# A gated decode step: gate moved into the attention output, MLP part added in PSUM, result copied by two engines and stored from two tiles

## The chip, the cores and the metric

The kernel runs on one core of a Trainium2 chip. The metric is device time in microseconds (us) of one execution; lower is better. Each quoted time is the median of a kernel's runs. Times inside an execution are counted from the start of its profile's span, which is some 1.8 us shorter than the device time of the same run.

## The reference

One decode step for 8 batch rows. Two branches are mixed by a gate per row:

```python
x = A_x                                               # [8, 1, 448]
g = sigmoid((x * gate_w).sum(-1, keepdims=True))      # one gate per batch row
a = attention(x, last 1024 keys and values) @ wo      # 16 query heads, 8 kv heads, width 256
b = gelu(layernorm(x) @ w1 + b1) @ w2 + b2
return g * a + (1 - g) * b
```

Almost all of the time goes into reading the keys and the values: 8 rows x 8 heads x 1024 x 256 in bf16, 33.6 MB each, and some 10 MB of weights.

## The kernel before

The cache is processed in 16 units `u`, one for each batch row and half of the kv heads. SyncE loads keys and values through a ring of 9 buffers of 2 MB. What the change touches lies at the start (gate), in `finish` (one small copy for each unit) and in the end after the last keys. Some words used below: PSUM is the memory in which TensorE adds up its products, and a bank is one of the pieces that it is divided into. A semaphore is a counter by which an engine or a DMA tells others that it has finished. A transfer is issued by an engine's queue and lands, that is, has finished, some time later.

```python
def norm_and_gate():
    ...                                             # gg[:, 0] = g, gg[:, 1] = 1 - g, on 8 partitions
    gp = ps_misc.tile([P, 2], F32, tag="misc", name="gp")
    nc.tensor.matmul(gp[:], lhsT=spread[:].rearrange("p i b -> p (i b)"), rhs=gg[:], start=True, stop=True)
    nc.vector.tensor_copy(gg_s[:], gp[:])           # both gates at partitions 32*i + b, i = 0..3

def finish(u):                                      # once for each unit
    ...                                             # two float32 matmuls into sm
    nc.scalar.copy(oT[...], sm[:])                  # L534

def mlp_out(hs):
    ...                                             # MLP output in bb, 4 column blocks at partitions 32*i
    nc.scalar.activation(mixb[:], bb[:], ACT.Copy, scale=gg_s[:, 1:2])   # (1 - g) * b, long before the end

# the end, u is the last unit
turn(u)                                             # VectorE transposes the probabilities: E -> ET
total(u)                                            # TensorE: den
invert(u)
nc.vector.memset(A_ps[:], 0.0)
...
spread_rows(0, HALF)                                # TensorE: pp; VectorE: oP
values(u)                                           # TensorE: PO <- ET, last value block
gather(u); finish(u)
project(0)                                          # 32 small matmuls into A_ps, column blocks at partitions 32*i
spread_rows(HALF, NHQ)
for q in range(1, NHQ):
    project(q)                                      # 96 more
nc.vector.scalar_tensor_tensor(                     # res = g * A_ps + mixb, all 128 partitions at once
    res[:], in0=A_ps[:], scalar=gg_s[:, 0:1], in1=mixb[:], op0=ALU.mult, op1=ALU.add)
for i, (src, cols) in enumerate(tiles(res)):        # 4 blocks of 8 rows x 112 columns
    eng = nc.sync if i % 2 == 0 else nc.scalar
    eng.dma_start(out_f[:, cols], src)
```

## Time and profile before

| | |
|---|---|
| Median device time | 190.97 us (190.83 to 191.34, 5 runs) |
| Span of the profile | 189.3 us |
| Loads | 77.7 MB |
| Projection's end to end of last store issue | 1.07 us |

(The ends of matmuls are modelled in a profile. By "projection's end" I mean, here and below, the start of the first instruction that reads the finished sum, 185.93 us in this profile.)

The page of the profile cuts the span into 40 slices; a digit is a busy share in tenths (9 is 90% or more), PEclk is the granted TensorE clock in tenths, and GB/s is what the DMA engines moved.

```profile
PEclk9999999999699966999955897999858999756955
DMA  5999999999999999999999999999999999999980
GB/s 188 422 424 434 428 435 431 422 422 440 429 433 429 426 436 426 429 436 433 429 426 433 428 436 422 433 433 426 436 426 433 436 426 426 436 433 426 410 356 14
```

The DMA row reads 9 from the second slice to the last but two, and still 8 (356 GB/s) in the last but one. This kernel is bound by its loads, so compute can be expected to cost time only at the start and at the end. The chain of waits that ended last says the same (shares of the span):

```profile
DMA 84%; PE 8%; DVE 3%; ACT 1%; SPq 1%; issue 1%; ACTq 0%
```

So the end has to be read instruction by instruction. In the timeline the columns are: start, duration (both us), engine, line, operation, output and inputs, shapes, count; in brackets the idle time before it and what ended it. (An engine's name with q is its sequencer: an issue or a wait, not work.)

```profile
178.50 0.21 ACT L534 CAST oT<-fin 128x16 bf16<-128x16 f32 x1
178.64 0.71 DVE L471 STREAM_TRANSPOSE ET<-E 128x512 int32<-128x512 int32 x1 [1.18 <-ACT E L458]
178.66 0.30 PEld L482 LDWEIGHTS den<-rowsum,rowden 128*128 128x128 f32 x2 [0.53 <-ACT E L458]
...
178.97 0.34 PE L656 MATMUL pp<-oT,ident 128*32 128x32 bf16 x16
...
179.40 1.04 PE L501 MATMUL PO<-slot,ET 128*16 128x512 bf16 x16
179.42 0.15 DVE L648 MEMSET A_ps<- 128x112 f32 x1
...
181.60 1.02 PE L531 MATMUL fin<-rsel,os__1552 128*128 128x8 f32 x4 [1.16 <-DVE os__1552 L516]
...
182.56 0.92 PE L672 MATMUL A_ps<-slot,oP 128*8 128x112 bf16 x32
...
183.41 2.46 PE L672 MATMUL A_ps<-slot,oP 128*8 128x112 bf16 x96
...
185.93 0.33 DVE L690 SCALAR_TENSOR_TENSOR res<-A_ps,gg_s,mixb 128x112 bf16<-128x112 f32 x1 [1.93 <-PE A_ps L672]
186.29 0.71 SPq L700 DMA_DIRECT2D out_dram<-res  x2
186.29 0.65 ACTq L700 DMA_DIRECT2D out_dram<-res  x2
```

The last value product (PO, 179.40) starts 0.05 us after VectorE has turned the probabilities (178.64 + 0.71). The projection (A_ps) runs from 182.56 to 185.9 without a gap. Then come one VectorE instruction of 0.33 us, and two stores on each of two queues, whose issue takes 0.3 to 0.4 us each. After that the stores land, SyncE waits for them and for everything else, and the program ends.

For the cost of the small copies I looked up the groups by line. Columns: minimum, median and maximum ns, first and last start.

```profile
L534 ACT CAST oT<-fin x16: 215/227/230, 51.7 to 182.7; 128x16 bf16<-128x16 f32 x16
```

SyncE's own waits at the end (line 726 is the end of the program; total us, number of waits, longest):

```profile
SPq L726 <- DMA out_dram<-res: 1.1, 2, 0.9
SPq L726 <- PEq L726: 0.7, 2, 0.5
```

### The profile page before, as it was taken

The page shows a single profiled execution, that of the slowest core. Times are in us where ns is not written, and L with a number is a line of the kernel's source. Part 1 is how long each engine was busy: PE and PEld are TensorE (multiplying, and loading weights), DVE is VectorE, ACT ScalarE, POOL GpSimd, SP SyncE. Part 2 cuts the span into 40 slices and gives each one's busy share as a digit, 9 for nine tenths or more (in the row PEclk, how much of TensorE's full clock was granted, in tenths as well). Part 3 has the DMA queues.
Part 4 walks back from the last instruction along what each step waited for, and adds up shares of the span by engine and source line. Part 5 has one row for each costly group of instructions (what it writes and reads, how often), then busy time and mean ns, then how long its engine had stood idle before and what let it go on. Part 6 is the DMA issues. An engine that isn't in the chain of part 4 may idle for free.

```text
span 189.3 us, 2502 instructions
## 1 busy us (share of the span) xinstructions
PE 134.2 (71%) x1013; PEld 69.8 (37%) x1022; DVE 128.1 (68%) x186; ACT 43.1 (23%) x91; POOL 5.0 (3%) x7
## 2 busy tenths in 40 slices
PE   0036899894878588866669985977499839399772
PEld 0021784441434143424225431533153414153461
DVE  7866266995949494949494949494958686772610
ACT  2031220313040404040401340314004404004510
POOL 8100000000000000000000000000000000000000
PEclk9999999999699966999955897999858999756955
DMA  5999999999999999999999999999999999999980
GB/s 188 422 424 434 428 435 431 422 422 440 429 433 429 426 436 426 429 436 433 429 426 433 428 436 422 433 433 426 436 426 433 436 426 426 436 433 426 410 356 14
DMA packets 6733, 77.84 MB, mean 411 GB/s; under 512 B 945, under 2 KB 1346, under 8 KB 1986
## 3 DMA queue, kind: packets, MB, share of 16 engines
q1 hardware_dynamic: 6512, 77.67, 96.5%
q8 instruction: 7, 0.11, 0.2%
q10 hardware_dynamic: 210, 0.02, 0.1%
q14 instruction: 4, 0.03, 0.0%
HBM read 77.68 MB, written 0.01 MB: 410 GB/s over the span
## 4 chain that ended last, share of the span: by engine, by line
DMA 84%; PE 8%; DVE 3%; ACT 1%; SPq 1%; issue 1%; ACTq 0%
DMA slot<-in_A_k_cache_dram 77%; DMA slot<-in_A_wq_dram 7%; PE S L429 3%; PE A_ps L672 2%; PE PO L501 2%; DVE kt L357 1%; PE fin L531 1%; ACT E L458 1%; SPq L118 1%; DVE mx L441 1%; ACT first L510 1%; DVE ET L471 0%; SPq L134 0%; PE mz L449 0%; DVE os__1552 L516 0%
## 5 line engine op out<-in xcount | busy, mean ns | idle before, releaser
L357 DVE STREAM_TRANSPOSE kt<-slot 128x2048 int32<-128x2048 int32 x32 | 73.7, 2306 | 33.7 <-DMA slot<-in_A_k_cache_dram 33.7
L429 PE MATMUL S<-kt,qw 128*128 128x512 bf16 x256 | 72.9, 433 | 30.5 <-DVE kt L357 26.7
L429 PEld LDWEIGHTS <-qw 128*128 128x128 bf16 x256 | 27.0, 106 | 69.4 <-issue 49.4
L458 ACT ACTIVATE E<-S,nmx 128x1024 bf16<-128x1024 f32 x16 | 22.2, 1387 | 2.6 <-DVE nmx L455 2.6
L534 ACT CAST oT<-fin 128x16 bf16<-128x16 f32 x16 | 3.6, 226 | 79.8 <-PE fin L531 79.8
L501 PE MATMUL PO<-slot,ET 128*16 128x512 bf16 x256 | 20.0, 441 | 0.1
L441 DVE TENSOR_REDUCE mx<-S 128x1 f32<-128x1024 f32 x16 | 19.0, 1187 | 0.3 <-PE S L429 0.3
L510 ACT ACTIVATE first<-PO,own 128x256 f32<-128x256 f32 x16 | 7.6, 473 | 29.2 <-PE PO L501 28.2
L471 DVE STREAM_TRANSPOSE ET<-E 128x512 int32<-128x512 int32 x16 | 11.2, 697 | 2.2 <-ACT E L458 2.2
L449 PE MATMUL mz<-m,same 128*128 128x4 f32 x32 | 6.8, 284 | 4.2 <-ACT oT L534 4.1
L423 PE MATMUL S<-place,foreign 128*128 128x512 bf16 x23 | 9.4, 409 | 0.1
L482 PEld LDWEIGHTS den<-rowsum,rowden 128*128 128x128 f32 x32 | 7.3, 234 | 3.9 <-issue 1.7
L449 PEld LDWEIGHTS mz<-m,same 128*128 128x128 f32 x32 | 5.7, 219 | 6.1 <-ACT oT L534 5.3
L501 PEld LDWEIGHTS <-ET 128*16 128x16 bf16 x256 | 5.3, 94 | 5.5 <-issue 2.3
L423 PEld LDWEIGHTS <-foreign 128*128 128x128 bf16 x32 | 3.2, 99 | 9.7 <-issue 7.9
L482 PE MATMUL den<-rowsum,rowden 128*128 128x1 f32 x32 | 5.2, 232 | 0.4 <-ACT E L458 0.4
L414 DVE CAST qw<-qp 32x512 bf16<-32x512 f32 x4 | 2.7, 687 | 3.4 <-ACT qw L412 3.4
L371 PE MATMUL Sq<-slot,xT 128*8 128x512 bf16 x32 | 3.9, 616 | 1.5 <-DMA slot<-in_A_wq_dram 1.5
L493 ACT ACTIVATE rsel<-sel,rb 128x8 f32<-128x8 f32 x16 | 4.7, 295 | 1.1 <-DVE rb L492 1.1
L455 DVE TENSOR_REDUCE nmx<-mz 128x1 f32<-128x4 f32 x16 | 2.3, 146 | 3.5 <-PE mz L449 3.5
L292 POOL MEMSET qw<- 128x5120 bf16 x1 | 4.4, 4364 | 0.0
L443 DVE TENSOR_SCALAR m<-block,mx 128x4 f32<-128x4 f32 x16 | 3.7, 229 | 0.6
(135 smaller groups left out, 84.9 us busy)
## 6 DMA issues: line engine op xcount, KB each, us to landing
slot<-in_A_v_cache_dram SPq DMA_DIRECT2D x16, 2048.0 KB, 36.5
slot<-in_A_k_cache_dram SPq DMA_DIRECT2D x15, 2048.0 KB, 38.8
slot<-in_A_wo_dram SPq DMA_DIRECT2D x3, 896.0 KB, 30.7
slot<-in_A_k_cache_dram SPq DMA_DIRECT2D x2, 1024.0 KB, 7.1
slot<-in_A_wq_dram SPq DMA_DIRECT2D x1, 2048.0 KB, 11.5
slot<-in_B_w_dram SPq DMA_DIRECT2D x1, 1568.0 KB
slot<-in_B_w_dram SPq DMA_DIRECT2D x1, 1344.0 KB
slot<-in_A_wq_dram SPq DMA_DIRECT2D x1, 1024.0 KB, 13.2
```

The costliest lines, as they stand in the source:

```text
L292: nc.gpsimd.memset(qw[:], 0.0)
L357: nc.vector.transpose(kt[:].rearrange("p c k x r -> p (c k x r)").bitcast(WORD), kn[:, hf * CH * Dh : (hf + 1) * CH * Dh].bitcast(WORD),)
L423: nc.tensor.matmul(S[u][:, cols], lhsT=foreign[:], rhs=place[:], start=True, stop=False)
L429: nc.tensor.matmul(S[u][:, cols], lhsT=qw[:, j, u, m * RQ : m * RQ + P], rhs=kt[:, :, k, :, par], start=False, stop=(k == NK - 1 and par = ...
L441: nc.vector.reduce_max(mx[:], S[u][:], axis=AXIS.X)
L449: nc.tensor.matmul(mz[:], lhsT=same[:], rhs=m4[:], start=True, stop=True)
L458: nc.scalar.activation(E[:].rearrange("p c x i -> p c i x"), S.pop(u)[:].rearrange("p (c i x) -> p c i x", i=PAIR, x=BLK), ACT.Exp, bias=n ...
L471: nc.vector.transpose(ET[:].rearrange("p c r i -> p (c r i)").bitcast(WORD), E[:].rearrange("p c x i -> p (c x i)").bitcast(WORD),)
L482: nc.tensor.matmul(den[u][:], lhsT=rowden[:], rhs=rowsum[:], start=True, stop=True)
L493: nc.scalar.activation(rsel[u][:], sel2[:], ACT.Copy, scale=rb[:])
L501: nc.tensor.matmul(PO[32 * t : 32 * t + PAIR * RQ], lhsT=ET[:, c, 0:RQ, :], rhs=vn[:, PAIR * c * Dh : PAIR * (c + 1) * Dh], start=(c < QUA ...
L510: nc.scalar.activation(first[:], PO[:, 0, :], ACT.Copy, scale=own[:, 0:1])
```

## The change

The intent: take the combining instruction out of the end. The gate is multiplied into the attention output while that is copied per unit anyway (a row's gate has to stand on all 128 partitions for this, hence the second small matmul at the start). The MLP's part is added by TensorE, as an identity matmul that opens the sum in `A_ps`. What is left at the end are copies; they are dealt out to two engines, and write two tiles of 8 rows, so that two stores are enough instead of four. Buffers of the MLP are shared to pay for the new constants, and the pad is cut so that the ring stays in its place.

```diff
+    each = consts.tile([NB, NB + P], F32); ident_f = consts.tile([P, P], F32)      # (two lines, shortened)
-    res = consts.tile([P, DO], BF16)
+    res = [consts.tile([NB, D // 2], BF16, name=f"res{i}") for i in range(2)]
 ... norm_and_gate: the gate of every row on all partitions
+        nc.vector.memset(each[:], 1.0)
+        nc.vector.tensor_scalar_mul(each[:, 0:NB], ident[0:NB, 0:NB], gg[:, 0:1])
+        nc.tensor.matmul(
+            gp[:, 1 : 1 + NB], lhsT=each[:, NB : NB + P], rhs=each[:, 0:NB], start=True, stop=True
+        )
 ... finish
-        nc.scalar.copy(oT[...], sm[:])
+        nc.scalar.activation(oT[...], sm[:], ACT.Copy, scale=gg_s[:, 1 + b : 2 + b])
 ... the end
-    nc.vector.memset(A_ps[:], 0.0)
+    nc.tensor.matmul(
+        A_ps[:], lhsT=ident_f[:], rhs=mixb[:], start=True, stop=False, skip_group_check=True
+    )
 ... project
-                    start=(q == 0 and j == 0),
+                    start=False,
 ... result
-    nc.vector.scalar_tensor_tensor(res[:], in0=A_ps[:], scalar=gg_s[:, 0:1], in1=mixb[:], ...)
-    for i, (src, cols) in enumerate(tiles(res)):
-        eng = nc.sync if i % 2 == 0 else nc.scalar
-        eng.dma_start(out_f[:, cols], src)
+    for i, (part, cols) in enumerate(tiles(A_ps)):
+        copy = nc.vector.tensor_copy if i < 2 else nc.scalar.copy
+        copy(res[i // 2][:, (i % 2) * DO : (i % 2 + 1) * DO], part)
+    for i, eng in ((0, nc.sync), (1, nc.scalar)):
+        eng.dma_start(out_f[:, i * D // 2 : (i + 1) * D // 2], res[i][:])
```

More of the change, by code (lines that the diff above doesn't have):

```diff
@@ L179, in slot @@
         return slots[index[key]]
-    consts.tile([P, 448], BF16, name="pad")
+    consts.tile([P, 16], BF16, name="pad")
     x_sb = consts.tile([NB, D], BF16)
@@ L228 @@
     spread = consts.tile([NB, OT, P // OT], F32)
-    gg_s = consts.tile([P, 2], F32)
+    gg_s = consts.tile([P, 1 + NB], F32)
+    ident_f = consts.tile([P, P], F32)
+    each = consts.tile([NB, NB + P], F32)
     ones_r = consts.tile([1, NB], BF16)
     mixb = consts.tile([P, DO], F32)
-    res = consts.tile([P, DO], BF16)
+    res = [consts.tile([NB, D // 2], BF16, name=f"res{i}") for i in range(2)]
     nc.vector.memset(spread[:], 0.0)
+    nc.vector.tensor_copy(ident_f[:], ident[:])
     nc.vector.memset(ones_r[:], 1.0)
@@ L340, in norm_and_gate @@
         )
-        gp = ps_misc.tile([P, 2], F32, tag="misc", name="gp")
+        nc.vector.memset(each[:], 1.0)
+        nc.vector.tensor_scalar_mul(each[:, 0:NB], ident[0:NB, 0:NB], gg[:, 0:1])
+        gp = ps_misc.tile([P, 1 + NB], F32, tag="misc", name="gp")
         nc.tensor.matmul(
-            gp[:],
+            gp[:, 0:1],
             lhsT=spread[:].rearrange("p i b -> p (i b)"),
-            rhs=gg[:],
+            rhs=gg[:, 1:2],
             start=True,
             stop=True,
+        )
+        nc.tensor.matmul(
+            gp[:, 1 : 1 + NB], lhsT=each[:, NB : NB + P], rhs=each[:, 0:NB], start=True, stop=True
         )
@@ L533, in finish @@
             )
-        nc.scalar.copy(
-            oT[:, half * RQ : (half + 1) * RQ, :, b].rearrange("p h j -> p j h"), sm[:]
+        nc.scalar.activation(
+            oT[:, half * RQ : (half + 1) * RQ, :, b].rearrange("p h j -> p j h"),
+            sm[:],
+            ACT.Copy,
+            scale=gg_s[:, 1 + b : 2 + b],
         )
@@ L571, in mlp_hidden @@
         nc.vector.tensor_tensor(z2[:], z[:], z[:], op=ALU.mult)
-        uu = consts.tile([P, NF, NB], F32)
+        uu = z2
         nc.vector.tensor_scalar(
@@ L579, in mlp_hidden @@
         nc.scalar.activation(th[:], w_[:], ACT.Tanh, scale=0.7978845608028654)
-        hh = consts.tile([P, NF, NB], F32)
+        hh = th
         nc.vector.tensor_scalar(hh[:], th[:], 1.0, 0.5, op0=ALU.add, op1=ALU.mult)
@@ L603, in mlp_out @@
         done()
-        nc.scalar.activation(mixb[:], bb[:], ACT.Copy, scale=gg_s[:, 1:2])
+        nc.scalar.activation(mixb[:], bb[:], ACT.Copy, scale=gg_s[:, 0:1])
     norm_and_gate()
@@ L675, in project @@
                     rhs=w[:, o + cols.start : o + cols.stop],
-                    start=(q == 0 and j == 0),
+                    start=False,
                     stop=(q == NHQ - 1 and j == NJ8 - 1),
+                    skip_group_check=True,
                 )
@@ L688 @@
         project(q)
-    nc.vector.scalar_tensor_tensor(
-        res[:],
-        in0=A_ps[:],
-        scalar=gg_s[:, 0:1],
-        in1=mixb[:],
-        op0=ALU.mult,
-        op1=ALU.add,
-    )
-    for i, (src, cols) in enumerate(tiles(res)):
-        eng = nc.sync if i % 2 == 0 else nc.scalar
-        eng.dma_start(out_f[:, cols], src)
+    for i, (part, cols) in enumerate(tiles(A_ps)):
[3 more added lines that the diff above has]
+        eng.dma_start(out_f[:, i * D // 2 : (i + 1) * D // 2], res[i][:])
 _INS = ['A_x', 'A_k_cache', 'A_v_cache', 'A_wq', 'A_wo', 'B_x', 'B_w1', 'B_b1', 'B_w2', 'B_b2', 'gate_w']
```

## The prediction

> **What bounds the kernel.** Loads. The slices of the page show the DMA engines 99% busy at 422 to 440 GB/s from the second slice to the last but one; 77.7 MB at about 430 GB/s is 181 us of the 189.3 us span. The chain of waits is 84% DMA; VectorE waits 33.7 us for keys (costliest groups). Up to the last key block (landed at 162.06 us) compute time is hidden, so the matter is the tail, read from the timeline: 162 to 180.5 compute on the last keys; last value product 179.41 to 180.47, which waits for the transposed probabilities (179.35); its split 180.56 to 181.54; `fin` 181.60; the output projection, 128 matmuls without a gap, 182.56 to 185.91; the combining VectorE instruction 0.33; four stores issued 186.29 to 187.00; 2.3 us until the span ends. The Trainium skill (DMA: Bandwidth & Descriptors, "Anatomy of one DMA") puts the fixed cost of a DMA at about 2.0 us; the trace agrees in size. Loads trickle until about 185 us (DMA in 40 slices of the last 7 us), so the projection has only about 0.6 us before it would wait for `wo`.
>
> **What the change does, in order of time.**
> 1. Start: two or three VectorE instructions (0.07 to 0.16 us each) and a float32 matmul of 8 rows (the one there took 0.56 with its two passes) before the first key transpose, 0.3 to 0.6 us. Key block 0 is freed later, but five or more blocks are queued at the DMA then: 0.
> 2. `oT` copies get a scale per partition. Plain copy 128x16: 0.227 us; scaled forms 128x8 0.295, 128x256 from PSUM 0.473, 128x112 0.353. Estimate from these: 0.27 to 0.29, so +0.05 each. PE waits for them 13 times (PSUM buffer), but in the load-bound part. In the tail one lies on the chain (169.14): +0.05. The last is hidden behind projection part 0.
> 3. The clear of the accumulator by VectorE (0.15, off the chain) becomes a float32 identity matmul 128x128 by 112 columns on TensorE, between the last `den` (ends 179.04) and the `pp` matmuls (0.34) and value product. Float32 weights take 0.19 each here, the matmul comes as two passes; estimate from `den` (0.36 to 0.42 per pair) and 112 columns more: 0.35 to 0.5. PE's slack there is about 0.09 us: +0.25 to +0.4 on the chain.
> 4. End: combining instruction (0.33) goes. Two ScalarE copies 8x112 from PSUM: estimate 0.227 + 96 elements at 0.83 ns (slope of 128x112 to 128x256) = 0.31 each, 0.6 together; VectorE's two about 0.45. So the slower store is issued 0.25 later, but each queue issues one store instead of two (0.30 to 0.37 each): the last issue ends about 0.1 earlier. Packets grow from 224 to 448 bytes, still under the 512 of the skill's table ("Specifications"), and are few: 0.
> 5. Smaller pad and shared buffers: memory only.
>
> Sum: +0.05 +0.33 -0.1 = +0.3 us. **Predicted 191.25 us, 190.5 to 192.0; faster by over 2% 0.01, within 2% 0.97, slower 0.02.**
>
> **What would show it.** Step 2: `oT` group at 0.27 to 0.29 mean, sum up about 0.9 us, DMA rate the same. Step 3: the new group between `den` and `pp`; last value product starts 0.25 to 0.4 later against `ET`. Step 4: from last projection matmul to last issue's end 1.0 instead of 1.09 us. The loads' end unchanged within 0.3 us.
>
> **What would make it wrong.** The granted clock halves at about 180.7 us, after a stretch of thin PE work; the added matmul could keep it full, and `fin` (1.02 against 0.61 at full clock) would win about 0.5 us, then capped by the loads of `wo`. Or the final DMA cost falls with two stores instead of four by more than the issue time; or ScalarE's small copies are dearer than estimated.

(Two passages are cut. One took the fixed cost of a DMA from a section that is about DMAs issued by GpSimd and said that the trace agrees; here SyncE and ScalarE issue, and the stores of the profile before landed 1.2 to 1.4 us after the start of their issue. The other gave a reason for the drop of the clock that no run tests. The table "Specifications" that step 4 names is in DMA: Bandwidth & Descriptors.)

## The result, and the profile after

The changed kernel takes 191.77 us (191.66 to 191.93, 5 runs) against 190.97 us: ratio 1.0041, 95% interval 1.0027 to 1.0056. (A ratio is the mean time of one kernel's fast runs over that of the other's of the same rounds, so not quite the ratio of the two medians.) It is slower by 0.8 us. That lies within the range of the prediction, but the shift is more than twice the 0.3 us that was forecast.

The same views after. First the slices; the loads are about as full as before (the last but one slice has 318 GB/s, before 356):

```profile
PEclk9999999999996999699985995589789995899555
DMA  5999999999999999999999999999999999999970
GB/s 200 429 411 420 445 419 430 442 431 431 414 431 442 438 425 418 438 431 435 431 421 430 431 438 431 431 418 431 438 428 435 421 431 435 431 433 413 419 318 3
```

The chain of waits is now almost wholly DMA, so the projection ended on a load and not on compute:

```profile
DMA 93%; DVE 4%; SPq 1%; issue 0%; PE 0%; ACT 0%; DVEq 0%; ACTq 0%
```

The timeline of the end:

```profile
175.10 0.32 ACT L542 ACTIVATE oT<-fin,gg_s 128x16 bf16<-128x16 f32 x1
175.24 0.71 DVE L479 STREAM_TRANSPOSE ET<-E 128x512 int32<-128x512 int32 x1 [1.18 <-ACT E L466]
...
175.26 0.38 PE L490 MATMUL den<-rowsum,rowden 128*128 128x1 f32 x2 [0.44 <-ACT E L466]
...
175.50 0.46 PE L659 MATMUL A_ps<-mixb,ident_f 128*128 128x112 f32 x2
...
175.88 0.34 PE L669 MATMUL pp<-oT,ident 128*32 128x32 bf16 x16
...
176.77 1.89 PE L509 MATMUL PO<-slot,ET 128*16 128x512 bf16 x16 [0.54 <-DMA slot<-in_A_v_cache_dram]
...
179.81 1.02 PE L539 MATMUL fin<-rsel,os__1557 128*128 128x8 f32 x4 [1.15 <-DVE os__1557 L524]
...
180.76 0.92 PE L685 MATMUL A_ps<-slot,oP 128*8 128x112 bf16 x32
...
181.62 0.93 PE L685 MATMUL A_ps<-slot,oP 128*8 128x112 bf16 x32
...
183.37 0.92 PE L685 MATMUL A_ps<-slot,oP 128*8 128x112 bf16 x32 [0.82 <-DMA slot<-in_A_wo_dram]
...
184.44 1.44 PE L685 MATMUL A_ps<-slot,oP 128*8 128x112 bf16 x32 [0.16 <-DMA slot<-in_A_wo_dram]
...
185.92 0.56 DVE L706 CAST res<-A_ps 8x112 bf16<-8x112 f32 x2 [3.71 <-PE A_ps L685]
186.51 0.36 SPq L708 DMA_DIRECT2D out_dram<-res  x1
186.57 0.50 ACT L706 CAST res<-A_ps 8x112 bf16<-8x112 f32 x2 [5.37 <-DVE res L706]
187.10 0.29 ACTq L708 DMA_DIRECT2D out_dram<-res  x1
```

Three things are to be seen. The added float32 matmul (L659, 175.50) is there, but the value product after it waits for something else: for the value block's load (0.54 us). Later the projection waits twice for its weights (0.82 and 0.16 us). And at the end ScalarE's two copies (186.57) do not run beside VectorE's two (185.92): they start when VectorE has finished, 0.65 us after the projection's end, and the bracket names VectorE as what they waited for. (ScalarE's records also have a wait for VectorE's semaphore, passed at 186.53.) (The work on the last keys was done some 3 us earlier than in the profile before. The granted clock from 160 to 170 us was 0.87 on average here and 0.67 there, which would fit, but no run tests this reason. As the loads end the projection, nothing came of it.)

The `oT` copies, and SyncE's waits at the end:

```profile
L542 ACT ACTIVATE oT<-fin,gg_s x16: 320/328/331, 50.4 to 180.9; 128x16 bf16<-128x16 f32 x16
```

```profile
SPq L734 <- DMA out_dram<-res: 1.4, 1, 1.4
SPq L734 <- PEq L734: 0.6, 2, 0.4
```

The mean rise of an `oT` copy is 0.10 us (median 227 to 328 ns). SyncE's waits for the stores changed in kind: two waits before, one after. To see why, I took the ends of all traces apart from their records of issues, of semaphore increments ("landed" is the last increment by a store) and of SyncE's waits:

| us | before | after |
|---|---|---|
| first copy starts (projection has ended) | 185.93 | 185.92 |
| from there to the end of the last store's issue | 1.07 | 1.47 |
| from there to the last store's landing | 1.09 | 0.92 |
| from the landing to the end of the span | 1.18 | 1.57 |
| span | 189.28 | 189.88 |

The projection ends at the same time in both. The whole of the loss is behind it: 0.40 us up to the last issue, and 0.39 us after the last landing, less 0.17 us in between, where the last store landed sooner after its issue. The second part I had not thought of at all.

It has a plain look in the records. At the end SyncE goes through a list of semaphore waits. Before: the first wait ended at 187.93, the second started at 188.12, 0.02 us after the last store had landed, and the rest followed at about 0.07 us each. After: the first ended at 188.35, just after the landing at 188.31; the next one, for a semaphore that had long been complete, started only at 188.79, 0.44 us later; then again 0.07 us each.

So there were these theories. A: the end is slower because ScalarE's copies wait for VectorE's, and the rest of the change is hidden. B: the new work on TensorE and ScalarE lengthens the chain, and one lucky profile hides it. C: the loads end later. For the step of 0.44 us: D, E and F below.

### The profile page after: what moved, and what is told of

Read it like the earlier page. It is cut to its first block, busy times and chain, and to the rows that moved or that the text cites. A ratio compares the mean times of both kernels' runs of the same rounds, so it can differ in the third digit from the quotient of the medians.

```text
span 189.9 us, 2523 instructions
## 1 busy us (share of the span) xinstructions
PE 137.3 (72%) x1026; PEld 70.1 (37%) x1026; DVE 128.7 (68%) x189; ACT 45.1 (24%) x93; POOL 5.0 (3%) x7
## 4 chain that ended last, share of the span: by engine, by line
DMA 93%; DVE 4%; SPq 1%; issue 0%; PE 0%; ACT 0%; DVEq 0%; ACTq 0%
DMA slot<-in_A_k_cache_dram 56%; DMA slot<-in_A_v_cache_dram 19%; DMA slot<-in_A_wo_dram 10%; DMA slot<-in_A_wq_dram 7%; DVE kt L365 2%; SPq L118 1%; DVE mx L449 1%; SPq L134 0%; DVE ET L479 0%; PE A_ps L685 0%; DVE os__1129 L524 0%; ACT res L706 0%; DVEq L734 0%; DVE res L706 0%; DVE m L451 0%
## 5 line engine op out<-in xcount | busy, mean ns | idle before, releaser
L542 ACT ACTIVATE oT<-fin,gg_s 128x16 bf16<-128x16 f32 x16 | 5.2, 328 | 74.8 <-PE fin L539 74.8
L431 PE MATMUL S<-place,foreign 128*128 128x512 bf16 x32 | 13.4, 418 | 0.2
L685 PE MATMUL A_ps<-slot,oP 128*8 128x112 bf16 x128 | 4.0, 290 | 1.2 <-DMA slot<-in_A_wo_dram 1.0
```

Source lines behind the costliest of these rows:

```text
L431: nc.tensor.matmul(S[u][:, cols], lhsT=foreign[:], rhs=place[:], start=True, stop=False)
L542: nc.scalar.activation(oT[:, half * RQ : (half + 1) * RQ, :, b].rearrange("p h j -> p j h"), sm[:], ACT.Copy, scale=gg_s[:, 1 + b : 2 + b],)
```

## The experiments

Twelve runs were made, all correct; e4 and e12 repeat a kernel. e1 to e8 ran on one chip, e9 to e11 on a second and e12 on a third, so results of different groups are compared by their ratios and not by their times. Ratios are to the kernel before in the same rounds; its medians were 190.91 us beside e1 to e4, 191.19 beside e5 to e8, 190.83 beside e9 to e11 and 190.77 beside e12. All ends, from the profile of each run:

| run | median us | ratio (95%) | projection end to last issue's end | landing to second wait of SyncE | landing to end of span |
|---|---|---|---|---|---|
| before | 190.97 | | 1.07 | 0.02 | 1.18 |
| after | 191.77 | 1.0041 (1.0027 to 1.0056) | 1.47 | 0.47 | 1.57 |
| e1 one copy, four stores | 190.69 | 0.9986 (0.9973 to 0.9999) | 1.02 | 0.02 | 1.04 |
| e2 such an end alone | 191.89 | 1.0050 (1.0038 to 1.0062) | 1.72 | 0.48 | 1.58 |
| e3 two banks | 191.20 | 1.0011 (0.9999 to 1.0023) | 0.94 | 0.47 | 1.57 |
| e4 after, again | 191.69 | 1.0040 (1.0027 to 1.0052) | 1.48 | 0.47 | 1.58 |
| e5 after, ten waits | 191.99 | 1.0039 (1.0023 to 1.0056) | 1.48 | 0.47 | 1.51 |
| e6 two banks, ten waits | 191.25 | 1.0010 (0.9994 to 1.0025) | 0.94 | 0.46 | 1.50 |
| e7 all copies on VectorE | 191.96 | 1.0044 (1.0028 to 1.0061) | 1.48 | 0.47 | 1.58 |
| e8 identity matmul three times | 191.08 | 0.9996 (0.9981 to 1.0011) | 1.01 | 0.02 | 1.03 |
| e9 two banks, one more issue | 190.69 | 1.0000 (0.9988 to 1.0013) | 0.93 | 0.02 | 1.10 |
| e10 after, one more issue | 192.21 | 1.0070 (1.0057 to 1.0082) | 1.48 | 0.02 | 1.10 |
| e11 one copy, one issue less | 191.08 | 1.0012 (0.9998 to 1.0025) | 1.02 | 0.27 | 1.33 |
| e12 one copy, again | 190.75 | 0.9999 (0.9986 to 1.0013) | 1.01 | 0.02 | 1.04 |

### e1: only the end undone

```diff
-    for i, (part, cols) in enumerate(tiles(A_ps)):
-        copy = nc.vector.tensor_copy if i < 2 else nc.scalar.copy
-        copy(res[i // 2][...], part)
-    for i, eng in ((0, nc.sync), (1, nc.scalar)):
-        eng.dma_start(out_f[:, i * D // 2 : (i + 1) * D // 2], res[i][:])
+    nc.vector.tensor_copy(res[:], A_ps[:])          # res is [P, DO] as before; pad 352, to keep the ring's place
+    for i, (src, cols) in enumerate(tiles(res)):
+        eng = nc.sync if i % 2 == 0 else nc.scalar
+        eng.dma_start(out_f[:, cols], src)
```

> The changed kernel with only its end undone: one VectorE copy of all 128 rows, then four stores, two on each queue; gate and MLP part stay where the change put them. Theory A (the loss is ScalarE's copies waiting for VectorE's, because both read one PSUM bank; the float32 matmul and the scaled copies are hidden behind the loads): from the last projection matmul to the end of the last issue about 1.0 us (0.27 copy, 0.03, 0.71 issues) against 1.48 in the changed kernel; 190.8 to 191.0 us, ratio to the kernel before 0.999 to 1.001. Theory B (the added TensorE and ScalarE work lengthens the tail and the one profile hides it): 191.2 to 191.4, ratio 1.001 to 1.003. Theory C (the loads end later because of the new start or the new memory layout): 191.1 to 191.3, with the last loads landing 0.3 us later than before.

Measured: 190.69 us, ratio 0.9986. With the gate in the attention output and the MLP part in PSUM, but the old end, the kernel is not slower than before. Theory B and theory C expected a loss of at least 0.1% and are out. (Against C the trace says the same: the last load landed at 185.19 us here and at 185.26 in the profile before; over the 14 profiles it lies between 185.19 and 186.00.) Its profile also fell in a run whose clock in the end was like that of the run before, so it shows directly what the added matmul costs there (timeline of e1):

```profile
178.60 0.71 DVE L479 STREAM_TRANSPOSE ET<-E 128x512 int32<-128x512 int32 x1 [1.17 <-ACT E L466]
...
178.62 0.38 PE L490 MATMUL den<-rowsum,rowden 128*128 128x1 f32 x2 [0.44 <-ACT E L466]
...
178.87 0.45 PE L659 MATMUL A_ps<-mixb,ident_f 128*128 128x112 f32 x2
...
179.40 0.38 PE L509 MATMUL PO<-slot,ET 128*16 128x512 bf16 x1
...
179.41 1.05 PE L509 MATMUL PO<-slot,ET 128*16 128x512 bf16 x15
...
185.88 0.28 DVE L704 CAST res<-A_ps 128x112 bf16<-128x112 f32 x1 [1.87 <-PE A_ps L685]
186.19 0.72 SPq L707 DMA_DIRECT2D out_dram<-res  x2
186.19 0.65 ACTq L707 DMA_DIRECT2D out_dram<-res  x2
```

The value product starts at 179.40, 0.09 us after the transpose's end (178.60 + 0.71), against 0.05 us before; it is 0.09 us in e4 and e10 too, where no load delayed this product either. So the matmul costs 0.04 us on the chain, although it is recorded with 0.45 us: it is done while VectorE transposes.

### e2: such an end put into the kernel before

```diff
-    nc.vector.scalar_tensor_tensor(res[:], in0=A_ps[:], scalar=gg_s[:, 0:1], in1=mixb[:], ...)
-    (four stores)
+    for i, (part, cols) in enumerate(tiles(A_ps)):
+        rows = slice(32 * i, 32 * i + NB)
+        nc.vector.scalar_tensor_tensor(res[i // 2][:, (i % 2) * DO : (i % 2 + 1) * DO],
+            in0=part, scalar=gg_s[rows, 0:1], in1=mixb[rows, :], op0=ALU.mult, op1=ALU.add)
+    for i, eng in ((0, nc.sync), (1, nc.scalar)):
+        eng.dma_start(out_f[:, i * D // 2 : (i + 1) * D // 2], res[i][:])
```

> The kernel before with only an end like that of the change: the combining instruction as four VectorE instructions of 8 rows into two tiles, one store for each, in series on VectorE. No gate in the attention output, no float32 matmul. Theory A: four in series of about 0.28 us and one issue of 0.36, about 1.5 us from the last projection matmul to the end of the last issue, as in the changed kernel, so 191.4 to 191.9 and a ratio of 1.0025 to 1.005: the loss is there without the rest of the change. Theory B: about 0.3 us less than the changed kernel at the same end. Theory C: no loss beyond what the end shows.

Measured: 191.89 us, ratio 1.0050: the loss comes with the end alone (timeline of e2).

```profile
185.99 1.39 DVE L692 SCALAR_TENSOR_TENSOR res<-A_ps,gg_s,mixb 8x112 bf16<-8x112 f32 x4 [3.59 <-PE A_ps L672]
```

The end was 1.72 us and not 1.5, because an instruction with three inputs on 8 rows took 0.32 to 0.34 us, as much as on 128 rows (0.33). The step of SyncE is there too.

### e3: two PSUM banks

```diff
+    A2 = ps_s.tile([P, W], F32, tag="S", name="A2")               # free by then; other banks than A_ps
+    acc = tiles(A_ps)[:2] + tiles(A2[:, 0:DO])[2:]
-    nc.tensor.matmul(A_ps[:], lhsT=ident_f[:], rhs=mixb[:], ...)
+    for half, dst in ((0, A_ps), (64, A2)):
+        nc.tensor.matmul(dst[half : half + 64, 0:DO], lhsT=ident_f[:, half : half + 64], rhs=mixb[:], ...)
     ... project and the copies go over acc instead of tiles(A_ps)
```

> The changed kernel with column blocks 2 and 3 of the projection accumulated in another PSUM bank (the identity matmul is done in two halves of 64 columns). Now ScalarE's copies wait for TensorE only. Theory A: both engines start at the last projection matmul, ScalarE's two copies end after 0.5 to 0.55 us, the last issue ends 0.9 to 0.95 us after the projection instead of 1.48, so 0.5 to 0.6 us faster than the changed kernel: 191.15 to 191.3, or 190.9 if the 0.2 us that the span grew after the last issue also go; ratio 0.999 to 1.002. Theories B and C: the copies overlap, but the ratio stays above 1.003 as the cost lies elsewhere.

Measured: 191.20 us. In the built program ScalarE's first copy had waited for VectorE's semaphore and TensorE's; now it waits for TensorE's alone, and the copies overlap (timeline of e3, VectorE and then ScalarE; `A` is `A2` without its number):

```profile
185.85 0.54 DVE L714 CAST res<-A_ps 8x112 bf16<-8x112 f32 x2 [3.63 <-PE A L693]
```

```profile
185.89 0.51 ACT L714 CAST res<-A 8x112 bf16<-8x112 f32 x2 [4.68 <-PE A L693]
186.43 0.30 ACTq L716 DMA_DIRECT2D out_dram<-res  x1
```

The last issue ends 0.94 us after the projection instead of 1.47. Theory A is right about the first half of the loss: it is this wait. That the wait comes from the shared bank fits, but e3 changed tile and bank together (`A_ps` lies in bank 7 of the built program, `A2` in bank 0), so whether the framework goes by the tile or by the bank no run separates. The Trainium skill (PSUM — Partial Sum Buffer, "PSUM bank collisions raise a hardware error") says that two engines collide on the same bank and the same quadrant of 32 partitions, reads with reads included, that different quadrants of one bank run clean, and that guarding by bank is the simple version of its rule. The four copies read four different quadrants; the framework of this kernel, which as I read it guards by bank, inserted a wait that the page's rule doesn't ask for. That the chip would have allowed the overlap inside one bank no run here shows.

But e3 is 0.5 us slower than e1 although its last issue ends at 186.78 against 186.91, and its last store lands at 187.86 against 187.99. The difference is after the landing: 1.57 us against 1.04. That is the step.

### e4: the changed kernel again

> The changed kernel unaltered, on this chip in the same rounds, for comparison and for a second trace: 191.7 to 191.9, ratio 1.003 to 1.0055. ScalarE's first copy again starts after VectorE's second has ended (about 0.65 us after the last projection matmul). By theory A the end of the projection lies at 185.9 within 0.3 us as before; the granted clock of the tail may differ from the first trace.

Measured: 191.69 us, ratio 1.0040; ScalarE again after VectorE, the step of SyncE again 0.44 us. This profile fell in a run where compute ended the projection, at 186.33. The projection's end scatters: over the 14 profiles it lies between 185.69 and 186.43, and in eleven of them between 185.8 and 186.0.

### e5 and e6: ten waits instead of eleven (a theory that fell)

In the built programs SyncE's list at the end has 10 waits, written as five pairs, where there are four stores, and 11 where there are two: one alone, then five pairs. Theory D blamed the lone wait. An idle matmul, read by VectorE after its copies, takes TensorE's semaphore off the list (the program of both confirms 10 waits in five pairs):

```diff
+    idle = ps_sm.tile([P, NB], F32, tag="sm", name="idle")
+    nc.tensor.matmul(idle[:], lhsT=ident[:], rhs=oP[:, 0, 0, :], start=True, stop=True)
+    junk = epool.tile([P, NB], F32, tag="nmx", name="junk")
+    nc.vector.tensor_copy(junk[:], idle[:])
     for i, eng in ((0, nc.sync), (1, nc.scalar)):
```

> The changed kernel with one thing more: after the last projection matmul TensorE does one idle 128x128x8 matmul and VectorE, after its two copies, reads it into a buffer that nobody uses. Nothing waits for either. The effect wanted is on SyncE's list of waits at the end of the program: in every version with two stores so far it has 11 waits, written as one instruction with one wait and five with two, and the step from the lone one to the next took 0.44 to 0.46 us after the last store had landed; the versions with four stores have 10 waits, five pairs. Here the list has 10. Theory D (the lone wait costs the 0.45 us): the gap goes, last landing to end of span 1.05 to 1.2 us instead of 1.57, 0.3 to 0.5 us faster than the changed kernel, about 191.3, ratio 1.001 to 1.003; ScalarE's copies still wait for VectorE's. Rival E (the extra time belongs to two stores of 448-byte rows or to the end in general): the gap stays between the first wait and the second, 191.6 to 191.9.

> The two-bank version with the same idle pair, so that both losses of the end are taken away: copies on both engines at once, and 10 waits. Theories A and D together: last store landed at about 187.9 as in the two-bank run, then 1.05 to 1.2 us to the end: 190.6 to 190.9 us, ratio to the kernel before 0.997 to 1.000, equal to or 0.1 better than the version with one copy and four stores. Rival E: as the two-bank version, 191.1 to 191.3.

Measured: 191.99 and 191.25 us, ratios 1.0039 and 1.0010, as without the pair. The step between the first wait and the second is still 0.44 us. Theory D is wrong.

### e7: all four copies on VectorE

```diff
-        copy = nc.vector.tensor_copy if i < 2 else nc.scalar.copy
+        copy = nc.vector.tensor_copy
```

> The changed kernel with all four copies on VectorE, two stores, 11 waits. Theory A says that ScalarE's part saved nothing, because it came after VectorE's: four copies in series 1.1 to 1.15 us, last issue's end about 1.5 us after the projection, as in the changed kernel: 191.5 to 191.9, ratio 1.003 to 1.005. If ScalarE had helped, this would be 0.4 us or more slower than the changed kernel.

Measured: 191.96 us, ratio 1.0044, end 1.48 us, as with ScalarE's help. Dealing the copies out to two engines bought nothing as long as ScalarE's waited for VectorE's.

### e8: the identity matmul three times

```diff
     (on e1)
-    nc.tensor.matmul(A_ps[:], lhsT=ident_f[:], rhs=mixb[:], start=True, ...)
+    for _ in range(3):
+        nc.tensor.matmul(A_ps[:], lhsT=ident_f[:], rhs=mixb[:], start=True, ...)
```

> The one-copy version with the identity matmul done three times in place (each one starts the sum anew, so the result is right). Measures what the matmul costs on the chain. If one such matmul is hidden (it is done while VectorE transposes the probabilities, and the value product starts 0.05 to 0.1 us after that transpose), then two more at 0.3 to 0.4 each push the value product 0.5 to 0.7 us past it: 190.9 to 191.4 us, the low end where the loads of the projection weights end last anyway. If a single one already lay fully on the chain (theory B), three cost three times its share and the one-copy version had hidden 0.3 us elsewhere: 191.3 or more in every run, with the first of them visibly delaying the value product.

Measured: 191.08 us, ratio 0.9996 (timeline of e8).

```profile
176.78 0.71 DVE L479 STREAM_TRANSPOSE ET<-E 128x512 int32<-128x512 int32 x1 [1.17 <-ACT E L466]
...
178.03 0.38 PE L509 MATMUL PO<-slot,ET 128*16 128x512 bf16 x1
```

The value product starts at 178.03, 0.54 us after the transpose's end (177.49), so two more matmuls cost 0.45 us on the chain, 0.23 us each. The projection then still waited for its weights (0.15 and 0.28 us) and ended at 186.00. A single one is hidden in front of the value product, and even three are mostly hidden behind the loads. The 0.46 us recorded for a single one lies within my estimate of 0.35 to 0.5, but the records overlap: what one more adds is half of that.

### e9, e10, e11: the place of the waits in SyncE's program

What else goes with two stores: SyncE's program has one instruction less before the end, 77 and not 78 (its main part as built). Theory F: the step belongs to a place in SyncE's stream of instructions, whatever stands there; rival E: to the 448-byte rows or the number of stores. e9 and e10 add one instruction by issuing an early load in two halves; e11 takes one away from e1 by letting ScalarE issue an early load.

```diff
     (e9 on e3, e10 on the changed kernel)
-    add(("w2",), rows_loader([w2_v]))
+    add(("w2",), rows_loader([w2_v[:, 0 : NF // 2 * D], w2_v[:, NF // 2 * D :]]))
     (e11 on e1)
-                nc.sync.dma_start(dst, ap)
+                eng = nc.scalar if ap is wq_t else nc.sync
+                eng.dma_start(dst, ap)
```

> The two-bank version with the load of w2 issued as two halves, so that SyncE's program before the end has one instruction more (78 as in the versions with four stores, not 77). Theory D has fallen: with ten paired waits the step of 0.44 us between the first wait and the second stayed. Theory F: the step belongs to the place of the instruction in SyncE's stream (the 78th to the 79th is where it waits, for its next instructions or otherwise); one instruction more puts the step before the first wait, where the stores are under way anyway. F expects the last landing to the end of the span at 1.05 to 1.2 us instead of 1.57, so 0.3 to 0.45 us faster than the two-bank version: 190.6 to 190.9 us, ratio 0.997 to 1.000. Rival E (the extra time belongs to stores of 448-byte rows, or to having two of them): the step stays, ratio 1.000 to 1.0025.

> The changed kernel with the same split of the w2 load and nothing else. Theory F: the step of 0.45 us between the first and the second wait of the end goes; what remains is ScalarE's copies after VectorE's (last issue's end 1.48 us after the projection): 191.2 to 191.4 us, ratio 1.001 to 1.003. Rival E: as the changed kernel, 191.6 to 191.9, ratio 1.003 to 1.005.

> The version with one copy and four stores, with one early load (the tail of wq) issued by ScalarE instead of SyncE, so that SyncE's program before the end has 77 instructions. Theory F: the step of 0.45 us appears between the first wait and the second although there are four stores of 224-byte rows and ten waits; as the last store lands only 0.2 us after the first wait, 0.2 to 0.25 us of it show: last landing to end of span 1.25 to 1.45 us instead of 1.04, ratio 0.3 per mille to 1 per mille above the one-copy version's 0.9986. Rival E: no step, as the one-copy version.

Measured: in e9 no step follows the landing, with two stores of 448-byte rows and eleven waits: the second wait starts 0.02 us after the last landing, and from there to the end of the span it takes 1.10 us instead of the 1.57 of e3. (The ratio falls from 1.0011 to 1.0000, but the intervals overlap, so the trace carries this.) In e11 the step of 0.44 us has come, with four stores of 224-byte rows and ten waits; as expected about half of it shows, because the last store lands in the middle of it. In SyncE's waits at the end (e3, e9, e11, then e12 as its control) a second wait for a store is one that was still open when SyncE came to it:

```profile
SPq L742 <- DMA out_dram<-res: 1.1, 1, 1.1
```

```profile
SPq L742 <- DMA out_dram<-res: 1.0, 2, 0.9
```

```profile
SPq L734 <- DMA out_dram<-res: 0.9, 1, 0.9
```

```profile
SPq L733 <- DMA out_dram<-res: 1.1, 2, 0.9
```

Rival E expected the step to stay in e9 and to stay away in e11, and is out. The other traces agree: in all eight that show the step, it lies between the 79th and the 80th record of SyncE, 0.44 to 0.45 us long. In the six others the 79th is the last store's issue and the 80th the first wait, which ends 0.9 us later as a store lands; a step there would not be seen, so it may be hidden and not gone. Theory F is shown as far as this: the step moves with one instruction more or less on SyncE, independent of stores and waits. What SyncE does in it isn't shown. The Trainium skill (Runtime: NRT & Kernel Launch, "Instruction fetch mechanics") says that an engine fetches its instructions in blocks by DMA, and that a taken branch to a page not at hand stalls; in the built program SyncE branches to the end just before its first wait. That would fit, but in none of the traces with the step does a read of the instruction queues fall into it, so the cause stays open.

e10 missed its expectation: 192.21 us instead of 191.2 to 191.4, in all five runs (191.99 to 192.26). No step follows the landing there either (second wait 0.02 us after the landing), but the landing itself is late: 1.92 us after the last issue's end instead of 0.92. The records show that seven of ScalarE's eight rows had started by 187.91; the eighth started only at 188.47, and its increment came 1.0 us after the others'. An 8,192-byte read of the instruction queue had started at 187.92 and took 0.555 us, so it ended when that row started. In e9 a read like it came as well, 0.5 us after all rows had been written. So in e10 a row of the store seems to have stood behind instructions being fetched; that both were on one DMA engine isn't in the records, so it is likely and not shown. In the changed kernel the same read came at 189.42, long after the stores; the shift seems to have brought it forward, and may have its own price.

### e12: the one-copy version again

> The one-copy version unaltered, once more, to see whether it really is at or below the kernel before (first time 0.9986, interval 0.9973 to 0.9999). Theories A and F: ratio 0.998 to 1.000, 190.6 to 190.9 us; from the projection's end to the last issue's end 1.05 us, no step between the first and the second wait of the end (the second starts when the last store lands), last landing to end of span 1.0 to 1.2 us. If the first result was luck: 1.000 to 1.0015.

Measured: 190.75 us, ratio 0.9999. The first 0.9986 was partly luck: e1 equals the kernel before within about 0.1%. By the ratios it is 0.4 to 0.5% faster than the changed kernel. No version beat the kernel before beyond doubt: e1 and e9 are the best, and both level with it.

## Why the prediction was right or wrong

The forecast time, 191.25 us in 190.5 to 192.0, holds the measured 191.77, and "within 2%" was right. The sum behind it was not: two errors of opposite sign, and a part that was missing. That the time fell into the range is partly luck.

- **What bounds the kernel**: right. The loads run at full rate to about 182.5 us in both. That the projection has little room before it would wait for `wo` was right too, and mattered more than I let it: in the profile after it did wait, and the projection's end did not move (185.93 and 185.92). The room was smaller than 0.6 us: in the profile after, the projection ended 0.43 us after the last part of `wo` had landed (185.49); before, that landed at 185.26, which leaves about 0.24 us by this estimate.
- **Step 1, the start ("0")**: right. The first key transpose began at 13.44 instead of 12.89 us and the loads did not notice.
- **Step 2, `oT` copies ("+0.05 each")**: mechanism right, size wrong. They rose from 0.227 to 0.328 us, so +0.10, about 1.6 us in all, and nothing of it reached the time (e1). The Trainium skill (ScalarE: Activation LUTs, "What ACT_TABLE_LOAD costs") has the figure: each operand given per partition adds about 93 ns. The trace agrees in size (0.10; the profile names the plain copy CAST and the scaled one ACTIVATE, so not only the operand changed); I had fitted a slope through other shapes instead.
- **Step 3, the identity matmul ("+0.25 to +0.4 on the chain")**: wrong in size. It was 0.04 us (e1). I had taken the recorded durations of the matmuls before it as if they followed each other, and so saw a slack of 0.09 us. They overlap: with three of them in a row (e8) each adds 0.23 us and not its recorded length.
- **Step 4, the end ("the last issue ends about 0.1 earlier")**: this step failed. It took for granted that ScalarE's two copies run beside VectorE's two. They ran after them, and the last issue ended 0.40 us later. The durations were near: 0.56 us for VectorE's two (forecast 0.45), 0.50 for ScalarE's two (forecast 0.6). What was missing was ScalarE's wait for VectorE, 0.65 us: with it taken out the last issue ends after 0.94 us (e3), and with all four copies on VectorE after 1.48, no later than in the changed kernel (e7).
- **"2.3 us until the span ends" taken as fixed**: the missing part. With one store less on its queue SyncE's list of waits moved by one place, and a step of 0.44 us came after the last landing (e9, e11); before, it would have fallen where SyncE waits for the stores anyway.
- **"What would make it wrong"** named the clock, a cheaper landing with two stores, and dearer ScalarE copies. None of them is the cause. In e1, with the added matmul, the clock halved at 180.55 us, in the profile before at 180.56; the landing came 0.17 us sooner after its issue, outweighed by the 0.39 us behind it; ScalarE's copies took 0.25 us each (forecast 0.31).

With the terms as measured, 0.40 us up to the last issue, -0.17 to the landing and 0.39 behind it make 0.62 us, about the 0.60 us between the two profiled runs (191.66 and 191.06). The medians differ by 0.8. I put the rest down to the scatter of single runs and to a last drain on TensorE that was 0.13 us longer in the profile before than in e1 (most of the table's 1.18 against 1.04); a second profile of the kernel before, which could show it, was not taken.

## What to carry to other kernels

Before two engines share the copies out of one accumulator, look at what makes them wait: reads of one PSUM bank may be put in series by the framework, and then one copy of all 128 rows (0.28 us) beats four of 8 rows (0.25 to 0.28 each), because the time of a copy hardly depended on the number of rows here. Work added to the end counts only as far as it outlasts what is awaited there, so compare starts with the end of the awaited thing, and don't add up recorded durations. At gains below half a microsecond the end of the program is itself part of the measurement: a store more or less changes when the last wait is passed, and a variant should be judged with its last landing and not only with its time.

## What the Trainium skill lacked or had wrong

- PSUM — Partial Sum Buffer: it gives the rule by bank and quadrant, but not what the simple version by bank costs: here 0.53 us at the end (last issue 1.47 us after the projection in one bank, 0.94 in two).
- DMA: Bandwidth & Descriptors: the fixed cost of about 2.0 us is fitted to the software path, on which GpSimd issues; the page has no such sum for the other path. The small stores here, issued by SyncE and ScalarE, landed 1.2 to 1.45 us after the start of their issue where nothing stood before them (in the profile after 1.24 and 1.21 us, in e3 1.44 and 1.26).
- DMA: Bandwidth & Descriptors has no figure for how long an instruction read can hold up a store, if that is what happened in e10 (likely, not shown): the last row started 0.55 us after the others, when an 8,192-byte instruction read ended, and landed 1.0 us late.
- Runtime: NRT & Kernel Launch: instructions are said to come in blocks of 16 KiB; the traces show reads of 16,384 bytes on one instruction queue and of 8,192 bytes (besides a few under 100) on the other.
- No page has the step of 0.44 us that SyncE takes at one place of its stream near the end of the program, nor that the program's own waits and drains take 1.04 us (e1) from the last landing to the last instruction without it.
